# Chunked attention and a Fourier mixer: the second weight's combination sums move from VectorE to GpSimd, and one pause of the weight rounding is dropped

## The chip, the cores and the metric

The kernel runs on one core of one Trainium2 chip. The metric is the device time of one execution in microseconds. Where several executions are timed, their median is given. The profile is of one execution of its own, and its time is given beside its span.

## The reference

Two blocks follow each other. The first is attention inside chunks of 64 tokens: q, k and v are 8 batches x 8 heads x 576 tokens x 64, and each chunk attends only to itself. Its output, laid out as x of 8 x 576 x 512, goes into a Fourier mixer with a two-layer network behind it:

```python
scores = scale * np.matmul(q_c, k_c.transpose(0, 1, 2, 4, 3))
attn = softmax(scores);  x = np.matmul(attn, v_c)       # per chunk of 64
mixed = np.real(np.fft.fft(np.fft.fft(x, axis=1), axis=2))
u = x + mixed
un = (u - mean(u)) / np.sqrt(var(u) + 1e-06)            # over the 512 features
out = u + np.maximum(un @ w_ch1, 0.0) @ w_ch2           # 512 -> 2048 -> 512
```

The two weights arrive as 64-bit floats and are rounded to 32 bits in the kernel.

## The kernel before

Tokens are worked in tiles of 128. A batch has four tiles and half of a fifth: two low tiles (LO), two high tiles (HI) that hold the mirrored tokens, and a rest tile (RE) that it shares with its neighbour. Four tiles are a group, so there are nine groups: one for each batch, and one of the four rest tiles. Group g is the network's work for batch g.

TensorE runs the network of the groups one after another (`mlp`): an up part that makes the hidden layer `h1`, and a down part that makes the output. Each is a generator that yields after a small piece of TensorE work, and the main loop counts these yields as `t`. In group 0 the up part is yields 1 to 16 and the down part 17 to 32, one yield for each of the 16 row blocks of a weight. Between the yields the loop writes the work of the next batch into the instruction streams: `sides[cur]` is attention and then `fourier` of batch `cur + 1`, cut into steps by its own yields, and `due` says how many steps have to be done by then. The order within each engine's queue is this program order. Nothing is moved by a scheduler.

Three other streams are put in by the same loop.

**Rounding.** The two weights come in 32 pieces of 512 KB: 16 of the first (`w1`), then 16 of the second (`w2`). `round_weight(i)` does the head of piece i (two VectorE instructions, L322 and L325, and three ScalarE activations, L314, L317, L320) and the tail of piece i-1 (three VectorE instructions, L335 to L337), and then starts the load of the next piece (L299) into the raw space that was freed. The raw spaces 0 and 1 are the tile `yall`, 2, 3 and 4 lie in `xall`. From piece 26 on (`N_LAST`) only 2, 3 and 4 are used. `n_w` is the number of the next piece. A step of `sides` that yields a true value is "heavy", and no piece is rounded in that turn:

```python
if not heavy:
    round_next()
    if t <= 2 or t < KF and t % 4 == 0 or t >= KF + 3:
        round_next()
```

**Sums of the second weight (`keep2`, called `conv2`).** From group 1 on the down part works with seven half-size products, from group 2 on the up part too. They need sums of the weights' quarters. A set of `keep2` makes four sums of 128 x 512 (L1017) and sends seven slabs of 256 KB to a DRAM scratch (L1021, `s<-...` in the profile). There are four sets, of five steps each. Sets 0 and 2 put their sums in `yall`, sets 1 and 3 in rows 8 to 11 of `xall`.

**Sums of the first weight (`keep1`, `conv1`).** The same for `w1`, on GpSimd (L999, stored at L1003), in group 1.

The loads of the later attention tiles (`load`, L203, for q and k; `load_v`, L226), the stores of results (L977, L986), the loads of weight pieces and the slabs of both `keep` functions are all issued from SyncE's one queue, SP. A DMA that has to wait holds up all that is behind it there. `att_T` transposes q and k of a tile on VectorE (L366); on the LO tiles GpSimd then copies one column (L368). `att_S` multiplies them (L398), `softmax` and `exponential` work on that (L411, L413, L424), `att_P` transposes the result (L347), `att_V` multiplies by v (L448) and scales into `xall` (L461 to L465).

`fourier(b)` makes the z products of a batch (L669), joins them (`z_joined`, L699 and L703), brings them into order (`z_tile`, `z_rest`) and makes three mixed tiles (L788) one after another: the rest tile, then i = 0, then i = 1. Each goes through ScalarE (L793), VectorE (L798, L799), a sum onto x (L805: VectorE for LO and rest tiles, GpSimd for HI tiles) and the statistics (L652, L653, L656, L657). `normed` (L940 to L944) and `turned` (L347, L957) then prepare the next group for TensorE.

Of the kernel before, what the change touches and what calls it, by code (L numbers as in the profile page):

```python
# [16 lines left out]
def kernel(  # L17
# [32 lines left out]
    nc = tc.nc  # L50
# [10 lines left out]
    KF = DFF // 128  # L61
# [84 lines left out]
    N_LATE, N_EARLY, N_LAST = 5, 8, 26  # L146
# [123 lines left out]
    def turn_dim_tables():  # L270
# [9 lines left out]
    pieces = [  # L280
        (w1[:, kk, f:f + 512], w_ch1[kk * 128:(kk + 1) * 128, f:f + 512])
        for f in range(0, DFF, 512)
        for kk in range(KD)
    ] + [(w2[:, m, :], w_ch2[m * 128:(m + 1) * 128, :]) for m in range(KF)]
# [376 lines left out]
    def z_sets(z, pm, i, turn_, first=False):  # L661


        for s in range(2):
            for q_ in range(4):
                k, r = (q_ // 2 + turn_) % 2, q_ % 2
                T, p = 2 * k + s, slice(32 * q_, 32 * q_ + 32)
                d0_ = T * HQ if i < NM else s * HQ
                nc.tensor.matmul(  # L669
                    out=z[r][k][:, s * NE:(s + 1) * NE], lhsT=pm[i][p, d0_:d0_ + HQ],  # L670
                    rhs=tk[p, NM - 1 - i if i < NM else NM, k],
                    start=first and s == 0, stop=False, skip_group_check=True,
                )

    def mid_products(outs, pm, i):
        p, m0 = (slice(0, 128), DM) if i < NM else (slice(CH, 128), 2 * HQ)
        for g, out_ in enumerate(outs):
            c0, c1 = halves[g % 2]
            nc.tensor.matmul(
                out=out_[:, 0:c1 - c0], lhsT=pm[i][p, m0 + g // 2:m0 + g // 2 + 1], rhs=tk[p, NM - 1 - i if i < NM else NM, 0, c0:c1],  # L680
                start=False, stop=i == NM, skip_group_check=True,
            )

    def z_space():


        odd = [ps_t.tile([128, 512], FP32, tag="pt", name="z") for _ in range(2)]
        even = ps_a.tile([128, 2, 512], FP32, tag="att", name="more_z")
        zs[1:] = even, odd
        return odd, [even[:, k] for k in range(2)]  # L690

    def z_odd():
        for k in range(2):
            nc.scalar.copy(zs[0][:, 2 * k:2 * k + 2, 1], zs[2][k][:, 0:2 * NE].rearrange("p (t f) -> p t f", t=2))
# [10 lines left out]
    def z_middle(outs):  # L705
        for g, out_ in enumerate(outs):
            c0, c1 = halves[g % 2]
            nc.scalar.copy(middle[:, g // 2, c0:c1], out_[:, 0:c1 - c0])
# [33 lines left out]
    def fourier(b):  # L742
        h = b % 2
        zf = one_p.tile([128, 4 * NL + 16], FP32, tag="zf", name="zf")
        zf = zf[:, 0:4 * NL].rearrange("p (t f) -> p t f", t=4)
        zs[0] = one_p.tile([128, 8 * NE], FP32, tag="two", name="zs").rearrange("p (t r f) -> p t r f", t=4, r=2)
        pm = [pms.pop((b, i)) for i in range(NM + 1)]


        z = z_space()  # L750
        for i in range(NM + 1):
            z_sets(z, pm, i, 0, i == 0)
        outs = [z[0][0][32 * g:32 * g + 1, 2 * NE:] for g in range(4)]
        for i in range(NM):
            mid_products(outs, pm, i)
        nc.scalar.copy(middle[:, 0, 0:1], outs[0][:, 0:1])
        yield b == 1
        if b == 1:
            yield
        mid_products(outs, pm, NM)  # L760
        for i in range(NM):
            z_sets(z, pm, i, 1)
        z_middle(outs)
        z_odd()
        if b == 1:
            z_joined()
        else:
            yield
            z_joined()
        nc.scalar.copy(zs[0][0:1, 2], middle)  # L770
        if h == 1:
            z_rest(h)
        for i in range(NM):
            z_tile(zf, i)
        if h == 0:
            z_rest(h)
        yield b == 1

        def mixed(i):
            mix = ps_t.tile([128, 512], FP32, tag="pt", name="mix")  # L780
            zt = zr.rearrange("p t h f -> p t (h f)") if i == NM else zf[:, :, 128 * i:128 * (i + 1)]
            for T, (cols, tab) in enumerate((
                (slice(0, HM + 1, 2), ce),
                (slice(1, HM, 2), co),
                (slice(0, DM, 2), cx),
                (slice(HM + 1, DM, 2), so),
            )):
                nc.tensor.matmul(  # L788
                    out=mix[:, cols], lhsT=zt[:, T], rhs=tab,
                    start=(T == 0), stop=(T == 3), skip_group_check=True,  # L790
                )
            y = three_p.tile([128, XW], FP32, tag="y", name="y")
            nc.scalar.copy(y[:, 0:HM + 1], mix[:, 0:HM + 1])  # L793
            nc.scalar.copy(y[:, DM:DM + 1], mix[:, 0:1])
            return y, mix

        def both(y, mix):
            nc.vector.tensor_tensor(out=y[:, DM - 1:HM:-1], in0=y[:, 1:HM], in1=mix[:, HM + 1:DM], op=ALU.subtract)  # L798
            nc.vector.tensor_tensor(out=y[:, 1:HM], in0=y[:, 1:HM], in1=mix[:, HM + 1:DM], op=ALU.add)  # L799
            return y  # L800

        def added(y, n):
            x, w = xt(n), DM + (kind(n) == HI)
            eng = nc.gpsimd if kind(n) == HI else nc.vector
            eng.tensor_tensor(out=x[:, 0:w], in0=y[:, 0:w], in1=x[:, 0:w], op=ALU.add)  # L805

        for i in ((NM,) if h == 1 else ()) + tuple(range(NM)):
            y = both(*mixed(i))
            ns = [rests[b // 2]] if i == NM else [at[LO, b, i], at[HI, b, i]]
            for n in ns:  # L810
                added(y, n)
            means(ns)
            yield
# [192 lines left out]
    def keep2(i):  # L1006

        m = 2 * i
        b11, b12 = w2[:, m:m + 2, 0:HM], w2[:, m:m + 2, HM:DM]
        b21, b22 = w2[:, HF + m:HF + m + 2, 0:HM], w2[:, HF + m:HF + m + 2, HM:DM]  # L1010
        to = xall[:, 2 * G:2 * G + 4, 0:DM] if i % 2 else yall
        o1, o2, o3, o4 = (to[:, j].rearrange("p (m e) -> p m e", m=2) for j in range(4))
        for out_, in0, in1, op in (
            (o1, b12, b11, ALU.subtract), (o2, b22, o1, ALU.subtract),
            (o3, b22, b12, ALU.subtract), (o4, b21, o2, ALU.subtract),
        ):
            nc.vector.tensor_tensor(out=out_, in0=in0, in1=in1, op=op)  # L1017
            yield
        to = s2.rearrange("o p (m e) -> o p m e", m=HF)
        for o, a in enumerate((b11, o2, o1, o3, b21, b22, o4)):  # L1020
            nc.sync.dma_start(out=to[o, :, m:m + 2], in_=a)  # L1021
        yield
# [217 lines left out]
    with tc.manual_schedule():  # L1240
# [22 lines left out]
        n_w = 2  # L1263
# [45 lines left out]
            for gen in gens:  # L1309
                yield from gen  # L1310

        n_conv = 0
        conv2, conv1 = chain(conv2), chain(conv1)
        t = 0
        for g in range(NG):
            for _ in mlp(g):
                t += 1
                heavy = False
                if t == 8:
                    nc.scalar.copy(tk, early_tk[:, :, :, 0:NE])  # L1320
                if cur < len(sides):
                    t0 = 3 if cur == 0 else ready_at[cur - 1]
                    t1 = ready_at[cur]
                    due = min(sizes[cur], (t - t0) * sizes[cur] // (t1 - t0))
                    while done < due:
                        heavy = next(sides[cur], None) or heavy
                        done += 1
                    if t >= t1:
                        for _ in sides[cur]:
                            pass  # L1330
                        cur, done = cur + 1, 0
                if not heavy:
                    round_next()
                    if t <= 2 or t < KF and t % 4 == 0 or t >= KF + 3:
                        round_next()

                if n_w > len(pieces) and t >= KF + 7:
                    for _ in range(3):
                        next(conv2, None)
                if t == begin[1] - 1:  # L1340
                    for _ in conv2:
                        pass
                if begin[1] <= t < begin[1] + KF // 2:
                    for _ in range(3):
                        next(conv1, None)
                if t == begin[1] + KF // 2:
                    for _ in range(NS2):
                        fetch(2)
                if t == begin[1] + KF:
                    for _ in range(NS1):  # L1350
                        fetch(1)
# [49 lines left out]
```

## Time and profile before

| | us |
|---|---|
| median of 3 runs | 1092.85 (1089.65 to 1093.28) |
| the profiled execution | 1090.81 |
| its span | 1089.0 |
| TensorE busy in the span | 1056.8 (97%) |
| VectorE busy | 590.6 (54%) |
| ScalarE busy | 309.5 (28%) |
| GpSimd busy | 308.4 (28%) |
| mean granted TensorE clock | 0.994 |

The profiled execution took 1.8 us more than its span. TensorE's busy time is the sum of its matmul records, which overlap, so the idle time is read from the gaps that the timeline marks and not from the share. One row of a matmul group counts two records for each instruction of the 512-wide products: "x8" is four matmuls, one yield of the loop in group 0's down part, 3.4 us.

### The profile page before, as it was taken

The page shows a single profiled execution, that of the slowest core. Times are in us where ns is not written, and L with a number is a line of the kernel's source. Part 1 is how long each engine was busy: PE and PEld are TensorE (multiplying, and loading weights), DVE is VectorE, ACT ScalarE, POOL GpSimd, SP SyncE. Part 2 cuts the span into 40 slices and gives each one's busy share as a digit, 9 for nine tenths or more (in the row PEclk, how much of TensorE's full clock was granted, in tenths as well). Part 3 has the DMA queues.
Part 4 walks back from the last instruction along what each step waited for, and adds up shares of the span by engine and source line. Part 5 has one row for each costly group of instructions (what it writes and reads, how often), then busy time and mean ns, then how long its engine had stood idle before and what let it go on. Part 6 is the DMA issues. An engine that isn't in the chain of part 4 may idle for free.

```text
span 1089.0 us, 19740 instructions
## 1 busy us (share of the span) xinstructions
PE 1056.8 (97%) x7410; PEld 840.4 (77%) x7410; DVE 590.6 (54%) x1287; ACT 309.5 (28%) x730; POOL 308.4 (28%) x459
## 2 busy tenths in 40 slices
PE   8999998789999999999999999999999999999998
PEld 6645454335888888888888888888888888888887
DVE  4899979134456555574456555745664534323421
ACT  4787463111203230223023312331134103101300
POOL 4301001356413341163306240535152401220140
PEclk9999999989999999999999999999999999999999
DMA  8776535688566826794568356874663355446232
GB/s 172 227 211 176 152 105 179 194 273 276 196 189 198 235 96 187 208 245 151 169 202 237 118 180 177 232 194 155 176 206 102 143 180 172 127 153 212 78 116 78
DMA packets 147949, 192.65 MB, mean 177 GB/s; under 512 B 66285, under 2 KB 104173, under 8 KB 140687
## 3 DMA queue, kind: packets, MB, share of 16 engines
q1 hardware_dynamic: 144204, 187.98, 57.2%
q10 hardware_dynamic: 3330, 2.76, 1.0%
q8 instruction: 59, 0.97, 0.3%
q0 software_dynamic: 320, 0.66, 0.3%
q14 instruction: 36, 0.29, 0.1%
HBM read 167.22 MB, written 24.12 MB: 176 GB/s over the span
## 4 chain that ended last, share of the span: by engine, by line
PE 82%; DMA 5%; DVE 5%; SPq 3%; ACT 3%; issue 1%; POOL 0%; DVEq 0%; ACTq 0%; POOLq 0%
PE pb L1190 20%; PE pa L1141 17%; PE pa L1190 15%; PE pb L1141 12%; PE up L1074 4%; PE dn L1095 3%; PE pt L347 2%; DMA wb<-s 2%; PE z L669 2%; PE mix L788 2%; PE xp L448 1%; SPq L216 1%; PE sc L398 1%; PE up L1054 1%; DMA out_dram<-o 1%
## 5 line engine op out<-in xcount | busy, mean ns | idle before, releaser
L1141 PE MATMUL pa<-unT,wa 128*128 128x256 f32 x672 | 159.9, 381 | 1.3 <-DVE wa L1149 1.3
L1141 PEld LDWEIGHTS pa<-unT,wa 128*128 128x128 f32 x672 | 126.2, 190 | 19.2 <-DVE wa L1149 1.8
L1042 POOL TENSOR_TENSOR h<-h 128x256 f32<-128x256 f32 x64 | 55.3, 870 | 230.6 <-DVE wb L1040 137.6
L1190 PE MATMUL pa<-wb,h 128*128 128x256 f32 x512 | 115.7, 380 | 0.0
L1190 PE MATMUL pb<-wb,h 128*128 128x256 f32 x512 | 114.9, 379 | 0.0
L1141 PE MATMUL pb<-wa 128*128 128x256 f32 x448 | 106.6, 381 | 0.0
L1190 PEld LDWEIGHTS pa<-wb,h 128*128 128x128 f32 x512 | 96.0, 190 | 13.0
L1190 PEld LDWEIGHTS pb<-wb,h 128*128 128x128 f32 x512 | 96.3, 190 | 12.6
L1141 PEld LDWEIGHTS pb<-wa 128*128 128x128 f32 x448 | 84.3, 190 | 11.5
L1147 DVE TENSOR_TENSOR wa<-pb,wa 128x256 f32<-128x256 f32 x56 | 23.8, 425 | 69.4 <-ACT wa L1146 69.4
L1095 PE MATMUL dn<-wb,h 128*128 128x512 f32 x128 | 57.5, 597 | 2.6 <-ACT h L1065 2.6
L505 POOL COPY xall<-xall 1x512 f32<-1x512 f32 x28 | 17.3, 620 | 149.7 <-DVE xall L465 120.4
L1074 PE MATMUL up<-unT,wa 128*128 128x512 f32 x128 | 59.1, 615 | 0.0
L1190 PE MATMUL pb<-wb,yall 128*128 128x256 f32 x256 | 58.2, 381 | 0.0
L1190 PE MATMUL pb<-wb 128*128 128x256 f32 x256 | 57.7, 379 | 0.0
L1190 PE MATMUL pa<-wb,yall 128*128 128x256 f32 x256 | 57.6, 379 | 0.0
L1146 ACT COPY wa<-pa 128x256 f32<-128x256 f32 x56 | 20.9, 373 | 123.3 <-PE pa L1141 87.3
L1141 PE MATMUL pa<-wa 128*128 128x256 f32 x224 | 53.9, 383 | 0.0
L1141 PE MATMUL pb<-unT,wa 128*128 128x256 f32 x224 | 52.9, 379 | 0.0
L1190 PEld LDWEIGHTS pa<-wb,yall 128*128 128x128 f32 x256 | 48.0, 190 | 6.1
L1190 PEld LDWEIGHTS pb<-wb,yall 128*128 128x128 f32 x256 | 47.7, 190 | 6.3
L1190 PEld LDWEIGHTS pb<-wb 128*128 128x128 f32 x256 | 47.6, 190 | 5.9
(265 smaller groups left out, 1754.2 us busy)
## 6 DMA issues: line engine op xcount, KB each, us to landing
wb<-s SPq DMA_DIRECT2D x56, 1024.0 KB
wa<-s SPq DMA_DIRECT2D x196, 256.0 KB
xall<-in_moe_w_ch_dram SPq DMA_DIRECT2D x22, 512.0 KB
q<-in_q_dram SPq DMA_DIRECT2D x96, 112.0 KB
k<-in_k_dram SPq DMA_DIRECT2D x96, 112.0 KB
v<-in_v_dram SPq DMA_DIRECT2D x124, 64.0 KB
yall<-in_moe_w_ch_dram SPq DMA_DIRECT2D x10, 512.0 KB
s<-wb SPq DMA_DIRECT2D x20, 256.0 KB
```

The lines of the kernel that those rows point to most:

```text
L216: eng.dma_start(out=t[p0:p0 + np_], in_=src[b, :, c * CH:c * CH + np_, :].rearrange("h p d -> p h d"))
L347: nc.tensor.transpose(pt[:, j, :], src(j), ident)
L505: nc.gpsimd.tensor_copy(to, from_)
L669: nc.tensor.matmul(out=z[r][k][:, s * NE:(s + 1) * NE], lhsT=pm[i][p, d0_:d0_ + HQ], rhs=tk[p, NM - 1 - i if i < NM else NM, k], start=fir ...
L788: nc.tensor.matmul(out=mix[:, cols], lhsT=zt[:, T], rhs=tab, start=(T == 0), stop=(T == 3), skip_group_check=True,)
L1042: nc.gpsimd.tensor_tensor(out=h1[:, m, hi], in0=h1[:, m, lo], in1=h1[:, m, hi], op=ALU.subtract)
L1074: nc.tensor.matmul(out=up, lhsT=w1[:, kk, m * 128:(m + 1) * 128], rhs=unT[:, kk], start=(kk == 0), stop=(kk == KD - 1),)
L1095: nc.tensor.matmul(out=dn, lhsT=h1[:, m, s * 128:(s + 1) * 128], rhs=w2[:, m, :], start=(m == 0), stop=(m == KF - 1),)
L1141: nc.tensor.matmul(out=dst, lhsT=w[:, kk, r], rhs=rhs[o][:, kk], start=(o in (0, 1) and kk == 0), stop=(kk == 1), skip_group_check=True,)
L1146: nc.scalar.copy(a, dst)
L1147: nc.vector.tensor_tensor(out=b, in0=pbs[r][:, 0], in1=a, op=ALU.add)
L1190: nc.tensor.matmul(out=dst, lhsT=lhs[:, m], rhs=w[:, m], start=(o in (0, 2) and m == 0), stop=(m == HF - 1), skip_group_check=True,)
```

## The change

`fourier` of batch 1 had two heavy steps, the first z products and the joining with the ordering. Now only the empty step between them is heavy. The sums of `keep2` run on GpSimd instead of VectorE. And their first set no longer waits until all 32 pieces are rounded: five steps of it may be taken as soon as `n_w` is over 26. The other sets start when all pieces are rounded, as before, but without the bound `t >= KF + 7`.

```diff
@@ fourier(b)
         for i in range(NM):
             mid_products(outs, pm, i)
         nc.scalar.copy(middle[:, 0, 0:1], outs[0][:, 0:1])
-        yield b == 1
+        yield
         if b == 1:
-            yield
+            yield True
         mid_products(outs, pm, NM)
...
         if h == 0:
             z_rest(h)
-        yield b == 1
+        yield
@@ keep2(i)
             (o3, b22, b12, ALU.subtract), (o4, b21, o2, ALU.subtract),
         ):
-            nc.vector.tensor_tensor(out=out_, in0=in0, in1=in1, op=op)
+            nc.gpsimd.tensor_tensor(out=out_, in0=in0, in1=in1, op=op)
             yield
@@ the main loop
-        n_conv = 0
+        n_sum = 0
...
-                if n_w > len(pieces) and t >= KF + 7:
-                    for _ in range(3):
+                for _ in range(3):
+                    if n_w > len(pieces) or n_w > N_LAST and n_sum < 5:
                         next(conv2, None)
+                        n_sum += 1
```

Worked through the loop, the yields fall as follows. Pieces 26 and 27 are rounded at t = 20 in both kernels. Before, pieces 28 and 29 come at t = 22, 30 and 31 at t = 24, the last tail at t = 25, and the four sets at t = 24 to 30. After, pieces 28 and 29 come at t = 21, 30 and 31 at t = 23, the last tail at t = 24, set 0 at t = 20 and 21, and sets 1 to 3 at t = 24 to 28.

## The prediction

> **What bounds the kernel now.** I read the page first: TensorE is busy 97% of the span, so time can only be won where TensorE stands still. I then took TensorE's waits, longest first, and its timeline around the longest. Its columns are start, duration, engine, line, and in brackets the idle time before it with what ended that.
>
> ```profile
> PE sc L398 <- DVE rd L461: 10.1, 1, 10.1
> PE pt L347 <- ACT un L942: 3.6, 3, 2.0
> ```
> ```profile
> 125.54 10.57 PE L1095 MATMUL dn<-wb,h 128*128 128x512 f32 x24
> ...
> 207.93 0.66 PE L347 MATMUL pt<-ident,ex 128*128 128x128 f32 x4 [1.97 <-ACT ex L424]
> ...
> 222.75 1.13 PE L398 MATMUL sc<-kT,qT 64*64 64x64 f32 x32 [10.10 <-DVE rd L461]
> 223.82 12.82 PE L1074 MATMUL up<-unT,wa 128*128 128x512 f32 x24
> ```
>
> One stop of 10.10 us, one of 1.97 us shortly before it, and behind the long one 24 records that take 12.82 us where 24 of the same size take 10.57 us at 125.54: 2.25 us more. The table by stage gives a granted clock of 0.67 for 215 to 235 us. So one place costs 10.10 + 1.97 + 2.25 = 14.3 us. After it TensorE hardly stops: over 235 to 1000 us its idle time is 1.3 us. Who causes it is in VectorE's timeline and in SP's:
>
> ```profile
> 198.78 0.20 DVE L462 RECIPROCAL rd<-rd 128x8 f32<-128x8 f32 x1
> 205.13 0.76 DVE L465 TENSOR_TENSOR xall<-xp,rd 128x256 f32<-128x256 f32 x2 [6.15 <-DMA s<-xall]
> ...
> 221.62 1.08 DVE L366 STREAM_TRANSPOSE kT<-k 128x512 f32<-128x512 f32 x1 [13.37 <-DMA k<-in_k_dram]
> ```
> ```profile
> 134.92 11.43 SPq L299 DMA_DIRECT2D xall<-in_moe_w_ch_dram  x5
> 146.40 0.43 SPq L1021 DMA_DIRECT2D s<-wb  x1
> 172.83 1.30 SPq L1021 DMA_DIRECT2D s<-yall  x3
> ...
> 184.94 2.17 SPq L203 DMA_DIRECT2D k<-in_k_dram  x4
> ...
> 198.48 1.99 SPq L203 DMA_DIRECT2D q<-in_q_dram  x4
> ...
> 209.43 2.52 SPq L986 DMA_DIRECT2D out_dram<-o  x2
> 212.04 3.74 SPq L203 DMA_DIRECT2D k<-in_k_dram  x4
> ```
>
> The product waits for kT, kT for k, and the k load is issued only at 212.04. SP stood at L1021 from 146.8 to 172.8 us for the first sums, then pushed four sets of slabs, two tiles' loads and the stores of group 0 through one after another. The 1.97 us are the same queue: L465 writes rows of xall whose slab had not left. Meanwhile the DMA engines idle: their share is 0.27 over 130 to 165 us, 0.81 over 215 to 235.
>
> [...] the first line below is VectorE's and takes 0.42 us elsewhere; it ends just after GpSimd's.
>
> ```profile
> 256.58 1.38 DVE L1041 TENSOR_TENSOR yall<-wb,h 128x256 f32<-128x256 f32 x1
> ```
> ```profile
> 256.36 1.32 POOL L520 TENSOR_TENSOR sum<-xall 128x512 f32<-128x512 f32 x1 [0.19 <-DVE xall L465]
> ```
>
> [...] Here L999, of the same shape as the moved sums, takes 1.27 us on GpSimd and L1017 0.69 us on VectorE: 1.84. [...] the 2.60 us stop at 114.8 us is followed by matmuls at full speed.
>
> **The change part by part.** TensorE's order is unchanged, so each of its waits is looked at.
>
> *Set 0 early.* Its first sum needs yall, last read at 132.3 us; the other three need the tail of piece 25, at 138.2. They come beside the rounding[...]. From L1041 above (1.38 for 0.42) and its two successors (0.94 and 0.89 for about 0.42) I take 0.8 us lost to VectorE for each GpSimd sum, 4 x 0.8 = 3.2 us; copies of one row at 87 and 105 us cost less, about 0.2 us per us of GpSimd, which gives 1.0 for the four. VectorE waits 0.24 and 0.27 us for loads there, and ScalarE 0.23 us for z, so most goes through: z_joined, at 148.36, comes 1 to 3 us late; I take 2.3. Its seven slabs leave at 146.4, behind the last weight loads, instead of from 172.8: no wait at L1021, and 1.75 MB go where the DMA engines were idle.
>
> *The rounding of pieces 30 and 31* is now ahead of the rest tile's L793 instead of behind its statistics. ScalarE has three activations for each, 1.9 us a piece: L793 moves from 152.96 to about 156.8, the rest tile by 3.8 us. The third mixed product needs the rest tile's PSUM buffer: TensorE waits 1.1 us there. Mixed tile i = 0 hardly moves, since both roundings (5.2 us on VectorE) stood ahead of it before; behind the rest tile it now has one tail (1.9 us), and comes 0.3 us later (L798 at 161.6 instead of 161.25).
>
> *Sums of set 1.* Three of them stand ahead of GpSimd's two L805. Two can run from about 156 us, the third once piece 31's tail has read its space; 1.27 us later L805 is free, about when it is wanted. They exclude L337 of the tail and L805 of the rest tile: 1.2 us by the same 0.8 each, less what overlaps.
>
> So un (L942) comes 2.3 + 0.3 + 1.2 = 3.8 us later than its 171.4, and TensorE with it: the 1.1 us above and the longer waits at the mixed products lie inside this. The wait of 0.67 us for ex at 176.65 goes, since L411 and L413 no longer stand behind five of the sums. **Loss: 3.8 - 0.67 = 3.1 us**, between 0 and 5.
>
> *The rest of the sums.* Nine sums follow the second L805 (now at about 171 to 172.8): 9 x 1.27 + gaps and the qT copy L368 end near 185. L368, between them, is done by 182.3; its product, at 182.3 before, is now at 185. VectorE loses 16 x 0.69 = 11 us, which was hidden. On SP the q load of 178.79 moves to about 179.5, k of 184.94 to 185.5, both with over 4 us to spare; then no slabs are left. The v load (2.6 us), q at 190 instead of 198.48, the eight stores at 193 to 198, **k at 198 instead of 212.04**. The k loads of 212.04 and 232.45 took 9.6 and 4.5 us from first issue to use (L366 at 221.62 and 236.90), so kT is ready at 204 to 209; I take 207. It is wanted at 222.75 - 10.1 - 1.97 + 3.1 = 213.8: 7 us in hand. L465 at 202 finds its slab sent at about 186.
>
> *What is late next.* The sums of the first weight start a little earlier and their slabs (from 217.4) at about 200; k of 232.45 at about 213, wanted at 229.7; the slabs read back (250.85) at about 230, wanted near 258. None is late. The other engines stay at about half load.
>
> **Sum:** -10.10 - 1.97 - 2.25 + 3.1 = **-11.2 us**: 1090.8 -> 1079.6 for the profiled execution. That was 2.0 us under the median; I forecast 1080.5, between the two bases.
>
> **Rivals.**
> *A, the stop moves.* The slabs, loads and stores that must pass SP between 173 and 200 us, some 6.8 MB, need 227 GB/s; the stage table has 260 over 215 to 235 and 325 over 235 to 260. If kT is late by 3 to 6 us, that stop and part of the clock's loss stay: gain 5 to 8, time 1083 to 1087. For it: SP's DMAs use eight semaphores in turn, so each waits for the eighth before it. Against it: 7 us in hand.
> *B, no exclusion.* If sums and rounding hardly meet, the loss is 0 and the time 1076.5. The exclusion shown at 256 us speaks against it.
> *C, slower.* GpSimd becomes the bound. The k load that stands behind set 3 waits for the tenth sum (L368 among them). With d us a sum k is issued at about 173 + 10d, and its product, at 201, needs it 9 us earlier: late from d = 1.9. The next k, 20 us on in the queue, adds about 2.5 us. The gain of 11 is gone at 10d - 19 + 2.5 = 11, d = 2.8 us. At 3.2 us a sum: 1095. It decides if blocking by VectorE more than doubles the sums; L999 at 1.26 to 1.28 beside L411 and L413 speaks against it[...].
> *D, no effect:* set 0 stays stuck behind piece loads. The SP order has its slabs right after the last piece, issued by 146.4. Time 1090 to 1093.
>
> **Numbers.** Main case 0.68 (1077 to 1084), A 0.16, B 0.06, D 0.05, C 0.05. A measurement of this kernel can tell about 0.3%, 3.3 us: faster 0.89, same 0.05, slower 0.06. The range 1075 to 1088 takes in A and B.
>
> **What would show it.** After: no stop above 2 us between 195 and 235 and a granted clock near 1.0 there; L1021 for yall issued before 150; the k load near 198; L1017 on GpSimd near 1.3 us; L335 to L337 above 1 us at 139 to 143; un's wait at about 3 to 4 us. I am wrong if the sums take over 2 us, if kT still waits for k, or if a new stop after 235 gives the time back.

## The result, and the profile after

The changed kernel takes **1085.26 us** (median of six runs, 1083.16 to 1086.70), the kernel before, timed beside it, 1092.80: a ratio of 0.9929, 95% interval 0.9908 to 0.9950. It is faster by 7.5 us where 12.3 had been forecast. It lies in the stated range of 1075 to 1088, but above the main case of 1077 to 1084. The profiled execution took 1083.94 us with a span of 1082.2, against 1090.81 and 1089.0.

First the waits of TensorE after. The columns are the total, how often, and the longest.

```profile
PE mix L788 <- ACT zr L735: 4.4, 1, 4.4
PE pa L1141 <- DVE wa L1149: 2.5, 2, 1.8
PE sc L398 <- DVE rd L461: 1.4, 1, 1.4
```

The stop of 10.10 us has become 1.4, and a new stop of 4.4 us heads the list, at the first mixed product, where TensorE had waited 1.00 before. TensorE's timeline around both places, before and then after:

```profile
117.41 3.70 PE L1095 MATMUL dn<-wb,h 128*128 128x512 f32 x8 [2.60 <-ACT h L1065]
...
151.29 0.49 PE L788 MATMUL mix<-ce,zr 128*128 128x129 f32 x2 [1.00 <-ACT zr L735]
...
152.49 3.60 PE L1095 MATMUL dn<-wb,h 128*128 128x512 f32 x8
```
```profile
117.19 5.39 PE L1095 MATMUL dn<-wb,h 128*128 128x512 f32 x8 [2.57 <-ACT h L1065]
...
156.17 0.80 PE L788 MATMUL mix<-ce,zr 128*128 128x129 f32 x2 [4.42 <-ACT zr L735]
158.47 5.14 PE L1095 MATMUL dn<-wb,h 128*128 128x512 f32 x8
...
217.01 0.70 PE L398 MATMUL sc<-kT,qT 64*64 64x64 f32 x32 [1.43 <-DVE rd L461]
217.64 10.57 PE L1074 MATMUL up<-unT,wa 128*128 128x512 f32 x24
```

L398 starts at 217.01 instead of 222.75, 5.74 us earlier. The 24 records behind it take 10.57 us again, not 12.82, so a further 2.25 us is won there. The wait for ex (1.97 us) is gone. But eight records of dn, which take 3.6 to 3.7 us at full clock, took 5.39 at 117 and 5.14 at 158: in this execution the clock fell at two other places (0.95 over 96 to 130 us and 0.90 over 130 to 165, both 1.00 before). The one at 158 follows the new stop. The one at 117 lies ahead of everything that the change moves, behind a stop that both kernels have; the last section shows that executions of the same code differ there, so that it is not the change.

What made z late is seen where VectorE (before, then after) and GpSimd (after) stand side by side:

```profile
138.45 0.43 DVE L322 TENSOR_SCALAR wb<-xall 128x512 uint32<-128x512 uint32 x1 [0.24 <-DMA xall<-in_moe_w_ch_dram]
...
139.13 0.68 DVE L335 SCALAR_TENSOR_TENSOR wb<-xall,wb 128x512 f32<-128x512 uint32 x1
```
```profile
140.66 1.33 DVE L322 TENSOR_SCALAR wb<-xall 128x512 uint32<-128x512 uint32 x1 [0.36 <-DMA xall<-in_moe_w_ch_dram]
141.91 1.49 DVE L325 TENSOR_SCALAR power<-xall 128x512 uint32<-128x512 uint32 x1
143.33 1.75 DVE L335 SCALAR_TENSOR_TENSOR wb<-xall,wb 128x512 f32<-128x512 uint32 x1
...
215.87 1.08 DVE L366 STREAM_TRANSPOSE kT<-k 128x512 f32<-128x512 f32 x1 [8.65 <-DMA k<-in_k_dram]
```
```profile
140.44 1.26 POOL L1017 TENSOR_TENSOR yall<-wb,yall 128x512 f32<-128x512 f32 x1 [10.62 <-DVE wb L337]
141.67 1.45 POOL L1017 TENSOR_TENSOR yall<-wb 128x512 f32<-128x512 f32 x1
143.08 1.45 POOL L1017 TENSOR_TENSOR yall<-wb,yall 128x512 f32<-128x512 f32 x1
```

The three roundings take 0.42, 0.42 and 0.69 us without a neighbour. Here they take 1.33, 1.49 and 1.75, and each ends 0.3 to 0.6 us after a sum on GpSimd does. This lengthening beside a sum on GpSimd is what exclusion stands for here. The last line of the second fence is the transpose that still waits for k. SP's timeline says why:

```profile
152.13 1.75 SPq L1021 DMA_DIRECT2D s<-yall  x3
...
163.80 4.85 SPq L1021 DMA_DIRECT2D s<-xall  x3
...
190.75 6.31 SPq L226 DMA_DIRECT2D v<-in_v_dram  x4
...
199.34 1.21 SPq L977 DMA_DIRECT2D out_dram<-o  x2
...
206.20 3.50 SPq L203 DMA_DIRECT2D k<-in_k_dram  x4
```

The first slabs leave at 152 instead of 173, but the k load goes at 206.20, where it was 212.04 before and 198 in the forecast.

### The profile page after: what moved, and what is told of

It reads as the page before. It is cut to its first block, busy times and chain, and to the rows that moved or that the text cites. A ratio compares the mean times of both kernels' runs of the same rounds, so it can differ in the third digit from the quotient of the medians.

```text
span 1082.2 us, 19747 instructions
## 1 busy us (share of the span) xinstructions
PE 1057.6 (98%) x7410; PEld 841.1 (78%) x7410; DVE 586.8 (54%) x1271; ACT 309.4 (29%) x730; POOL 328.6 (30%) x475
## 4 chain that ended last, share of the span: by engine, by line
PE 81%; DVE 6%; DMA 6%; ACT 4%; SPq 2%; issue 1%; POOL 1%; DVEq 0%; ACTq 0%; POOLq 0%
PE pb L1190 21%; PE pa L1141 17%; PE pa L1190 15%; PE pb L1141 13%; PE pt L347 3%; PE up L1074 2%; PE dn L1095 2%; PE mix L788 2%; PE z L669 1%; PE sc L398 1%; PE xp L448 1%; PE up L1054 1%; DMA v<-in_v_dram 1%; DMA out_dram<-o 1%; DMA q<-in_q_dram 1%
## 5 line engine op out<-in xcount | busy, mean ns | idle before, releaser
L1095 PE MATMUL dn<-wb,h 128*128 128x512 f32 x128 | 60.8, 625 | 2.6 <-ACT h L1065 2.6
L1074 PE MATMUL up<-unT,wa 128*128 128x512 f32 x128 | 56.8, 596 | 0.0
```

The lines of the kernel that those rows point to most:

```text
L1074: nc.tensor.matmul(out=up, lhsT=w1[:, kk, m * 128:(m + 1) * 128], rhs=unT[:, kk], start=(kk == 0), stop=(kk == KD - 1),)
L1095: nc.tensor.matmul(out=dn, lhsT=h1[:, m, s * 128:(s + 1) * 128], rhs=w2[:, m, :], start=(m == 0), stop=(m == KF - 1),)
```

## The experiments

Each kernel was timed beside the kernel before, whose median on the same chips was 1091.5 to 1092.9 us. The question was which of the three parts brings the time, why the k load gained 6 us and not 14, and what the new stop costs.

**1. The sums on GpSimd alone** (`e1_pool_alone`). Both pauses and the late first set are those of before; only the bound on t is dropped.

```diff
-            nc.vector.tensor_tensor(out=out_, in0=in0, in1=in1, op=op)
+            nc.gpsimd.tensor_tensor(out=out_, in0=in0, in1=in1, op=op)
```

> Only the engine is changed: all 16 L1017 sums on GpSimd, pauses and start of the sums as before. Theory Q (the queue: the gain comes from SP no longer standing at L1021 and from set 0's slabs leaving early): SP still stands at L1021 until about 170, k of the stopped tile is issued at 206 to 212, TensorE's stop before L398 stays at 5 to 10 us, time 1087 to 1092. Theory R (relief: the gain is the 11 us of sums that VectorE no longer does): about as fast as the changed kernel, 1085.

Measured: 1090.74 us, ratio 0.9983 (0.9970 to 0.9995). The relief of VectorE is worth 1.7 us and no more. All 16 sums ran behind the two L805, from 170.19; SP stood at L1021 until 173.16 as before; the k load left at 211.37, and the stop stayed:

```profile
221.86 1.13 PE L398 MATMUL sc<-kT,qT 64*64 64x64 f32 x32 [9.75 <-DVE rd L461]
```

**2. GpSimd and the dropped pause** (`e2_pool_and_pause`): the edit of 1 and the three lines of `fourier`.

> Sums on GpSimd and the new pauses, but set 0 is not released early in the program order. Three of its sums then still stand ahead of the two L805 on GpSimd and run at 128 to 144 us, the fourth behind them. Theory Q: six of set 0's slabs leave at about 152, the last at about 176, everything behind it on SP some 4 us later than in the changed kernel: stop before L398 of 4 to 7 us, wait at the first mixed product 3 to 4.5 us, time 1087 to 1090. Theory R: 1085.

Measured: 1088.78 us, 0.9950 (0.9930 to 0.9970). With the rounding done sooner, three sums of set 0 ran at 128.25 to 142.8, the other 13 from 172.42; the mixed product waited 3.35 us. The k load left at 208.55 and L398 still waited 6.32.

**3. GpSimd and the early first set** (`e3_pool_and_early`): the change without the three lines of `fourier`.

> Sums on GpSimd and the early first set, with the old pauses (rounding of pieces 30 and 31 behind the rest tile's statistics again). Theory Q with exclusion: the wait at the first mixed product comes from the three sums at 140 to 144 us and not from the pauses, so it stays at 3.5 to 4.5 us with the clock's loss behind it; the end is within 1.5 us of the changed kernel, 1084 to 1087. Rival P (the new pauses cause it, by ScalarE's six activations ahead of L793): that wait is under 1.5 us and the time 1080 to 1082.

Measured: 1090.84 us, 0.9984 (0.9974 to 0.9995). The mixed product waited 4.78 us, so that stop comes from the early sums and not from the dropped pause. The rest was a miss: the time hardly moved. Set 0 left from 145.67, but set 1 is now held up behind both L805, and with it all that stands behind it on SP:

```profile
177.31 2.72 SPq L1021 DMA_DIRECT2D s<-xall  x3
...
211.53 3.50 SPq L203 DMA_DIRECT2D k<-in_k_dram  x4
```

In the full change these slabs left from 163.80. Dropping the pause has pieces 30 and 31 rounded early enough for three sums of set 1 to stand ahead of L805. Neither half gives the gain alone: with the sums on GpSimd in each, it is 3.6 us with the pause dropped, 1.6 with the early set (no more than GpSimd alone), 7.5 with both.

**4. The early set held until z is joined** (`e4_early_gated`): experiment 3, with a small GpSimd copy that reads the joined z ahead of set 0's sums, and set 0 not before t = 23.

```diff
+        if b == 1:
+            nc.gpsimd.tensor_copy(warm[:, 290:291], zs[0][:, 3, 1, 0:1])
...
-                    if n_w > len(pieces) or n_w > N_LAST and n_sum < 5:
+                    if n_w > len(pieces) or n_w > N_LAST and n_sum < 5 and t >= KF + 7:
```

> As e3, but one small GpSimd copy of a column of the joined z stands ahead of set 0's sums (taken from t = 23 on), so that they run only behind z_joined, while VectorE waits for the mixed tile. Theory Q with exclusion: L322, L325 and L335 at 140 to 145 us are back at 0.42 to 0.69 us, the wait at the first mixed product is 1 to 2 us, granted clock 1.0 over 130 to 165 us, set 0's slabs leave at about 152 to 156, stop before L398 under 3 us; time 1078 to 1082. Rival (exclusion costs nothing, z is late for another reason): wait at the mixed product still above 3 us, time 1084 to 1087.

Measured: 1087.44 us, 0.9943 (0.9920 to 0.9965). L322, L325 and L335 were back at 0.43, 0.42 and 0.68, z was joined at 148.06, the mixed product waited 0.99 with the clock at 1.00. So of the loss ahead of z the part in these roundings is the exclusion. The time was a miss again, and the reason is one number: k left at 206.88, so kT was no earlier than in the full change, and what TensorE had saved it waited at L398 (6.42 us at 218.20).

**5 to 7. The stores of group 0 behind the next loads.** The eight stores (199.34 to 206.1) stand right ahead of the k load. They are put off until t = 34, behind k and v, and with them four stores of the same group that go out on ScalarE's queue: in the changed kernel (`e5_late_stores`), in the kernel before (`e6_before_late_stores`) and in that of experiment 4 (`e7_gated_late_stores`).

```diff
-                    store(n, o)
+                    if g == 0:
+                        late.append((n, o))
+                    else:
+                        store(n, o)
...
+                if t >= 34:
+                    for _ in range(min(len(late), 99)):
+                        store(*late.pop(0))
```

> The changed kernel, and group 0's result stores (L977, L986) issued at t = 34 instead of in the loop's last down step, so that they stand behind the k load of the stopped tile and behind the next v load. Theory S (what is left of the stop is the eight stores ahead of k on SP and their slow landing): k issued at about 198, no wait over 1 us before L398 at 215, gain of 1.5 to 3 us over the changed kernel, 1082 to 1084. Rival B (the DMA engines' total work sets when k lands): the stop stays at 1 to 2 us, 1085.

> The kernel before, and only the stores moved as in e5. Theory S: k issued at about 205 instead of 212, lands within 5 us, the stop of 10.1 us before L398 falls to 0 to 3 us and the clock's loss behind it goes: 1080 to 1084, without any of the change's edits. Rival Q (the slabs of the sums ahead of k are the cause, the stores a small part): stop still 5 us or more, 1087 to 1090.

> e4 (sums on GpSimd, set 0 behind z_joined, old pauses) with the stores of e5. Theory S: e4's stop of 6.4 us before L398 falls below 2 us with the clock's loss behind it: 1078 to 1081, faster than the changed kernel. Rival B: stop of 4 us or more, 1085 to 1087.

Measured: 1088.37 us (0.9961, 0.9949 to 0.9973), slower than the change; 1092.96 (1.0005, 0.9991 to 1.0019), the same as before; 1086.53 (0.9952, 0.9932 to 0.9972). In all three the stop left its old place and came back one tile later, at 238.51 (5.44 us), 243.26 (8.98) and 232.84 (6.88). SP's and VectorE's timelines of the first show it (its profiled execution, like that of the second, was its longest):

```profile
219.99 4.25 SPq L203 DMA_DIRECT2D q<-in_q_dram  x4
```
```profile
231.10 1.10 DVE L366 STREAM_TRANSPOSE qT<-q 128x512 f32<-128x512 f32 x1 [10.76 <-DMA q<-in_q_dram]
```

The load that now stands behind the stores came 11.1 us after its issue. What k gains by going first, the next load gives back.

**8. Throwaway products ahead of the mixed product** (`e8_warm_mix`): the changed kernel, with ten products of 128x289 into the tile `mix`, which the first real product overwrites.

```diff
+            if b == 1 and i == NM:
+                for _ in range(10):
+                    nc.tensor.matmul(out=mix[:, 0:NQ], lhsT=warm[:, 0:128], rhs=warm[:, 0:NQ], start=True, stop=True, ...)
```

> The changed kernel with ten matmuls of 128 x 289 whose result is overwritten, put ahead of the first mixed product, so that TensorE works while it waits for the ordered z. If the clock's loss at 156 to 163 us comes from the length of the stop (4.4 us), the eight records after it take 3.6 us again instead of 5.14, the granted clock over 130 to 165 us is near 1.0, and the time falls by 2 to 2.6 us to about 1083. If the clock falls for another reason, nothing changes: 1085 to 1086.

Measured: 1082.13 us (1081.13 to 1083.18), 0.9904 (0.9886 to 0.9922). The eight records behind the mixed product took 3.60 us again; the clock still fell once, to 0.95 over 130 to 165 us, but while the throwaway products ran (20 records in 6.82 us; 16 in 4.16 in experiment 11, at 1.00). L398 began at 216.11, 0.9 us earlier than in the change. The interval still overlaps the change's (0.9908 to 0.9950), so that this is a gain over it is likely and not shown.

**9. The change without GpSimd** (`e9_pauses_and_early`): the pause dropped, the first set early, the sums on VectorE as before.

> The kernel after, but with its sums on VectorE as before: the pause dropped and the first set early, nothing on GpSimd. Theory V (the time came from the order on SP, and GpSimd is only another place for the same 11 us): the seven sums ahead of un cost VectorE 7 x 0.69 = 4.8 us where the exclusion cost it some 5; the slabs of set 1 leave at 163 to 169, the k load goes at about 206, the stop at L398 is under 3 us, the time 1083.5 to 1087, within 0.2% of the kernel after. Theory W (the move to GpSimd is needed): the nine later sums stand in VectorE's queue between statistics, softmax and transposes, ex and kT come late, the stop at L398 is over 5 us and the time 1087 to 1091.

Measured: 1084.11 us (1080.24 to 1087.47), 0.9924 (0.9903 to 0.9946). That is the ratio of the full change, 0.9929, within its interval of some 2 us on either side: the move to GpSimd brings nothing that can be measured once the two others are there. The pause or the early set alone, with the sums on VectorE, was not run. The profiled execution was this kernel's longest and 2.3 us behind at 117 already; in it the stop at L398 was 1.77 us.

**10. The change with the first set held** (`e10_pauses_gated`): the copy and the bound of experiment 4 in the full change, and four steps a turn instead of three while t < 25, so that three sums of set 1 keep their place ahead of L805.

```diff
-                for _ in range(3):
+                for _ in range(4 if t < KF + 9 else 3):
```

> The kernel after, but the first set of sums is held until z is joined (one small copy on GpSimd ahead of it), and up to four steps are taken in a turn, so that three sums of set 1 still stand ahead of L805. Theory X (the loss of 3 us at z_joined is the exclusion by the three sums, and the stop at L398 is held off by set 1's slabs, which need the dropped pause): L322, L325 and L335 return to 0.42, 0.42 and 0.69, the first mixed product waits under 2 us with no loss of clock behind it, set 1's slabs leave before 172, the stop at L398 stays under 3 us, the time is 1079 to 1083. Theory Y (the exclusion only moves to the roundings of pieces 30 and 31 and to the rest tile): un comes as late as in the kernel after, the time is 1084 to 1087.

Measured: **1079.72 us** (1079.38 to 1080.23), 0.9885 (0.9862 to 0.9908), the fastest kernel of the study; each of its four runs is under each of the six of the change, and beside the kernel before, at 1091.51 here, the gain is 11.8 us. TensorE's timeline:

```profile
151.51 0.49 PE L790 MATMUL mix<-ce,zr 128*128 128x129 f32 x2 [1.00 <-ACT zr L735]
...
160.73 0.77 PE L790 MATMUL mix<-ce,zf 128*128 128x129 f32 x2 [3.32 <-DVE y L801]
...
214.07 0.69 PE L398 MATMUL sc<-kT,qT 64*64 64x64 f32 x32 [1.35 <-DVE rd L461]
```

z is on time again (joined at 148.57). The exclusion is still there, on other roundings (L335 and L336 at 1.76 and 1.77 us, 0.68 and 0.69 at 145), but ahead of work that had more room:

```profile
150.78 1.76 DVE L335 SCALAR_TENSOR_TENSOR wb<-xall,wb 128x512 f32<-128x512 uint32 x1
152.47 1.77 DVE L336 SCALAR_TENSOR_TENSOR power<-xall,power 128x512 uint32<-128x512 uint32 x1
```

It now shows as 3.32 us at the third mixed product, behind which the clock fell too (0.95 over 130 to 165 us; 0.90 in the change), and i = 0's L798 is at 164.23 instead of 167.09. The second L805 ends 2.9 us earlier, hence the nine sums behind it, hence the k load (204.11). The stop at L398 is no longer than in the change, since both sides of it moved. Up to 1 us of this lead at L398 is not the edit's: the clock behind the stop at 117 stayed full here and fell in the profiled execution of the change. The edit has two parts, the held set and the four steps, and they were not run apart.

**11 and 12. Throwaway products ahead of group 0's first dn as well**: four there and eight ahead of the mixed product in the change (`e11_warm_both`), four there alone in the kernel of experiment 10 (`e12_gated_and_warm`).

> The kernel after with throwaway products into PSUM that nothing reads: four of 128x289 ahead of group 0's first dn, eight ahead of the first mixed product of batch 1. Theory C (part of what is lost is the granted clock behind the stops of 2.6 us at 117 and 4.4 us at 156): matmuls behind both at full speed, time 1079.5 to 1082.5, at or below the kernel with ten ahead of the mixed product alone (1082.13). If the four ahead of dn only add to TensorE's queue and the clock did not fall there: 1082 to 1084.

> The kernel with the held first set (1079.72), and four throwaway products of 128x289 ahead of group 0's first dn. Theory C2 (the granted clock falls behind the stop of 2.6 us at 117 in some executions, and filling it takes that away): clock 1.00 over 96 to 130, dn behind it at 3.70 for eight records, time 1078 to 1079.8. Theory Z (the stop does no harm in the version with the held set, which showed no loss of clock there): the same 1079.7 within 0.5, and the four products cost nothing since the stop is filled.

Measured: 1081.37 us (1079.87 to 1082.47), 0.9898 (0.9877 to 0.9918), and 1080.48 (1079.73 to 1084.77), 0.9891 (0.9870 to 0.9912). The stop of 2.57 us shrank to 0.43 in both, dn behind it took 3.70, and the granted clock over 96 to 130 us was 1.00. Against experiments 8 and 10 neither is a gain that can be told apart: filling that stop does no harm, and in the best kernel it brings nothing.

**What they say together.** In the kernels that leave the stores in place, L398's start follows the issue of its k load. The times are those of the profiled executions, the last column is the median of all executions; that of kernel 2 was profiled in its fastest, at 1085.02.

| kernel | k issued | L398 starts [stop] | between | median |
|---|---|---|---|---|
| before | 212.04 | 222.75 [10.10] | 10.7 | 1092.80 |
| 1, GpSimd alone | 211.37 | 221.86 [9.75] | 10.5 | 1090.74 |
| 3, with the early set | 211.53 | 222.01 [6.67] | 10.5 | 1090.84 |
| 2, with the dropped pause | 208.55 | 219.73 [6.32] | 11.2 | 1088.78 |
| 4, early set held | 206.88 | 218.20 [6.42] | 11.3 | 1087.44 |
| after | 206.20 | 217.01 [1.43] | 10.8 | 1085.26 |
| 10, change with set held | 204.11 | 214.07 [1.35] | 10.0 | 1079.72 |

Experiments 8, 9, 11 and 12 (k at 205.03, 209.46, 205.10 and 203.84) have 11.1, 10.6, 10.5 and 10.5 between. The length of the stop says little: kernels 2, 3 and 4 all have it at 6.3 to 6.7 us and differ by 3.4 us in time. It is the difference of two arrivals. The k load sets the end, and behind the five stops of 6.32 to 10.10 us the 24 records took 11.58 to 13.12 us for 10.57, 1.0 to 2.6 us more.

## Why the prediction was right, and where it was too high

The place, the mechanism and the side were right: SP's queue held the k load, the early departure of the first slabs freed it (together with the dropped pause, as 2 and 3 show), the wait for ex went, and the clock behind L398 came back. The size was not. Read against the kernel before, TensorE's lead is 5.74 us at L398, 8.08 at 240 and 6.8 at the end. The sum term by term, forecast and measured:

| term | forecast | measured |
|---|---|---|
| stop at L398 | -10.10 | -8.67 (1.43 is left) |
| wait for ex | -1.97 | -1.97 |
| clock behind the stop | -2.25 | -2.25 |
| loss ahead, at the product for ex at 181.82 (was 176.65) | +3.1 | +5.17 |
| later waits on L1149 | 0 | +1.2 |
| sum | -11.2 | -6.5; the profiled executions differ by 6.87 |

**The step that failed most is "k on SP at 198, 7 us in hand".** k left at 206.20, 8.2 us later. The first k load was 2.8 us late (188.27 for 185.5): the sums ended 1.1 us late, and the last slabs behind them took 2.2 us to issue where I had 0.5. The v load behind it took 6.31 us where I had put in the 2.6 of before. SP's waits from 187 to 200 us, before and then after, and ScalarE's queue after show why:

```profile
SPq L1021 <- DMA out_dram<-o: 3.8, 1, 3.8
```
```profile
SPq L226 <- DMA out_dram<-o: 2.6, 1, 2.6
```
```profile
194.73 2.44 ACTq L986 DMA_DIRECT2D out_dram<-o  x4
```

Four of group 0's stores are issued from ScalarE's queue and not from SP's. In the traces the DMAs of both queues count on the same eight semaphores in turn, and v's fourth load waits for the one that the store issued at 194.73 raises. Before, the same wait stood at the slabs ahead of v (5.02 us for three of them), so v itself took only 2.64. The forecast named the eight semaphores under rival A and put no wait for them into the sum. These stores come as group 0's last products are done, so they are as late as TensorE is: 190.30 before, 194.73 after. The loss ahead was therefore charged a second time, to k.

The stores on SP took 6.8 us instead of 5. From k's issue to a finished kT I had 9 us and it took 10.75 (206.20 to 216.95). kT was wanted at 217.01 - 1.43 = 215.58. The seven us were all used up, though un came later than I said and put off the moment at which kT was wanted. It does not follow that an earlier un would have left a longer stop: in experiment 10 the product for un came 2.85 us earlier (174.60), k left 2.09 us earlier, and the stop was 1.35.

The median is in rival A's band of 1083 to 1087, and it is in the range because the range took in A. A was right that kT would be late and that the reason lay on SP. It was not late by 3 to 6 us, and the bytes from which A was argued did not bind: the DMA engines' share over 195 to 215 us was 0.42. (A's sum has a slip as well: 6.8 MB in the 27 us from 173 to 200 are 252 GB/s, not 227.)

**The second is z_joined, 2.3 us late in the forecast and 4.88 in the trace** (153.24 for 148.36). Three sums cost VectorE 0.91, 1.07 and 1.06 us, where I had 0.8 each and expected part of it to vanish in waits; hardly any did. The first sum met L520 at 128.61, which took 1.77 us for 0.69: another 1.08. About 1 us came with the slow clock behind the stop at 117 (5.39 us for 3.70), which is no part of the change. Experiments 4 and 10 show the exclusion as the cause of the 3 us: held until z is joined, the roundings take their old time.

**The third is the clock behind the new stop, which the forecast put at nothing.** It had the loss as a wait of 3 to 4 us at un. The wait came at the first mixed product instead, 4.42 us, with 5.14 us for the eight records behind it that take 3.60 at full clock; un's own wait shrank from 2.04 to 0.51, so that most of this loss was absorbed there.

**What went as worked out.** un came 6.0 us late, which is 4.88 + 0.3 for the tail behind the rest tile + 0.8 for set 1 (the two L805 on VectorE at 1.32 and 0.86 for 0.69; I had 1.2). The sums behind L805 took 1.26 to 1.28 us and ended at 186.1 (185 in the forecast), so rival C, a GpSimd that becomes the bound, is out. The slabs of set 0 left at 151.6 to 156.9, so D is out; B is out by the exclusion. The clock over 195 to 235 was 1.00.

**What it did not ask.** Whether the move to GpSimd is needed at all: it was credited with the wait of 0.67 us for ex, and its alternative was not worked out. Experiment 9 shows that the other two parts do as well without it, and 10 that on GpSimd the first sums want a place behind the joining of z. The later waits on L1149 (2.5 us instead of 1.3) were not followed to their cause. They run from none to 2.5 us over the profiled executions, so that the 1.2 need not be the change's. They also account for what experiments 8, 10 and 11 gain on the change at the end beyond their lead at L398 (1.7, 1.7 and 1.4 us): there they are 1.3, 0.6 and 1.0 us.

## What to carry to other kernels

A stop is the difference of two arrivals, so follow the later of them: find the load that the waiting product needs and all that its queue waits for ahead of it, DMAs of other queues included, since the issue of that load, and not the length of the stop, told the time here. When a DMA took little time to issue right behind a long wait, ask whose wait that was: take away what waited, and the wait falls on the next DMA (2.6 us became 6.3 here). And work moved to GpSimd belongs where VectorE has no work that the exclusion hits (here the roundings, L322 from 0.42 to 1.33 us, and the sum L520, from 0.69 to 1.77) and the end depends on: the same first sums, held back by 10 us and taken four to a turn, gave some 5 us more.

## What the runs showed of the hardware

**Loads behind stores.** The load that stands right behind the eight stores (64 and 128 KB each) was used 8.8 to 11.1 us after its first issue, wherever the stores were put (k in experiment 10 at 8.8, counted back from L398's start as in the change, where it was 9.67; q in experiments 5, 6 and 7 at 11.1, 9.4 and 9.4), while loads with no stores ahead took 3.8 to 4.4 (k at 200.03 in experiment 7, q and k at 220.81 and 227.23 in the change). In the chain of waits of the changed kernel one such store lasts 10.63 us, 203.24 to 213.87. The DMA engines had room: their share over 195 to 215 us was 0.42. What in the stores makes it so was not tried.

**The clock after short stops.** The stop ahead of group 0's first dn was 2.56 to 2.62 us in the twelve profiled executions that have it unfilled, and eight records of dn behind it took 3.70 us in five and 5.39 to 6.73 in seven. Behind the stops at the first mixed product, 1.87 us was followed by 5.12 us for eight records (experiment 12) and 1.79 by 3.60 (experiment 9). So these stops cost 1.5 to 3 us more than themselves, or nothing. The one at 117 did either in executions of the same code up to there: 3.70 us before and 6.73 in experiment 6, behind stops of 2.60 and 2.58, and 5.39 in the change and 3.70 in experiment 8, behind 2.57 in both. So it was not the change that made the profiled execution of the change slow at 117.

What decides was not shown. In the trace of before, from 10 to 1070 us, the granted clock was 0.50 from 214.74 to 228.39 us, and in that of the change from 117.20 to 120.62 and from 154.75 to 161.58; elsewhere it was 1.00. These stretches of 13.65, 3.41 and 6.83 us, and the 34.13 us between the two of the change, are 4, 1, 2 and 10 times 3.413 us. If such steps run through the whole trace, the stop of 2.57 us in the change lies whole in the one from 113.79 to 117.20, and before, the 2.60 us are cut at 115.75 into 0.94 and 1.66. That the place of the stop in the steps decides is an estimate from these two traces alone. These lengths take the ends of the matmul records as they stand, and they are modelled.
